# Pooled attention and two MLPs: half of the plain products, a turn on VectorE and a shorter warm-up in group 0

## The chip, the cores and the metric

One core of a Trainium2 chip runs the whole program in one launch. The metric is the device time in microseconds (us), the median of several runs; three runs of the kernel before are shown. An engine is named by its profile name: PE is TensorE, DVE VectorE, ACT ScalarE, POOL GpSimd, SP SyncE, whose queue issues the DMAs.

## The reference

Inputs are float64 arrays. Attention has 8 batches, 8 heads, 576 positions and 64 columns; k and v are averaged over blocks of 8 positions, so 72 keys stay per head. Its output, 4608 rows of 512, goes through two MLPs with 2048 hidden columns:

```python
k_p = k.reshape(B, H, Sp, pool, D).mean(axis=3)
v_p = v.reshape(B, H, Sp, pool, D).mean(axis=3)
scores = scale * np.matmul(q, k_p.transpose(0, 1, 3, 2))
attn = np.exp(scores - np.max(scores, axis=-1, keepdims=True))
attn = attn / (np.sum(attn, axis=-1, keepdims=True) + 1e-09)
x = np.matmul(attn, v_p)
...
h = x @ w_in
g = h * (1.0 / (1.0 + np.exp(-h)))
x = g @ w_out
...
h = x @ w_in2
g = h * np.clip(h + 3.0, 0.0, 6.0) / 6.0
out = g @ w_out2
```

## The kernel before, in words

The 4608 rows are 36 tiles of 128 (TPG = 4 to a group), 9 groups of 512 (NG). The hidden columns are 16 slices of 128 (NF). The first MLP runs group by group and, in a group, slice by slice; one pass of that loop is called a slot here, slot f of group g. Everything is written in the order in which each engine executes it (manual_schedule); engines wait for each other only by data and buffers.

A slot of the first MLP does h_mm (L489: twelve products of 128x512, since x and the weight are each held as a high and a low part), the activation act_a (L507: tanh on ACT, then one DVE pass), and y_mm of the slice before (L546: twelve products again, high and low parts). For that, act_b (L523) splits g into gh (ACT) and gl (DVE). In group 0 the kernel takes another way for y: g and the weight of w_out stay whole in float32, and y_whole (L536) does four plain float32 products; the weights of w_out are then split in group 1 by split_whole (L137).

The weights arrive as float64. split_a (L101) makes a float32 of each: ACT copies, then DVE does a shift and one or two passes of two operands; with mul the last step is POOL's and ACT adds a sign. split_b (L144) makes the high part (ACT) and the low part (POOL subtracts). There are 32 pieces, w_in and w_out of each slice in turn; five are converted before slot 0, and this table says how many in each slot:

```python
share = [2, 2, 2] + [1, 3, 2] * 4 + [2]
```

In a slot, one conversion stands right behind act_a and the rest of the quota further back, behind y_mm and ahead of norm in program order (L862, L864).

The attention of the next group's four tiles runs in the slots of a group; stages (L670) says where. Step 1 is scores (L349, PE), below_max (DVE), exps (ACT) and, late in the slot, norm (L403, DVE). The probabilities must then be turned so that keys stand on partitions. In group 0 step 2, a slot later, is probs_T (L414): eight PE transposes and two ACT copies. In all later groups step 4 in the slot of the scores is vector_T (L431): three DVE transposes of 32x32 blocks, a write of 384 KB to DRAM and three reads back in the order wanted; SP issues them at the start of the next slot (the list later). Step 3 is weighted (L456, PE) and split_x: two slots behind the scores in group 0, three in the others. In group 0 the scores stand in slots 3, 6, 9 and 12 (tiles 4 to 7), in later groups in slots 0, 4, 8, 12.

pool_k (L277, DVE) and pool_v (L297, POOL) add up blocks of 8; batch 1's k, which tile 4 needs, is pooled in slots 0 to 2. The buffer of v serves for the turned blocks too (tag v).

Before slot 0 the four tiles of group 0 go through attention alone. PE first runs products on zeros: warm_wide (L332), 14 of 128x512, 10 of 128x256 and 10 with another stride, then keep_warm with WARM[t], pairs of 128x128 ahead of the scores and the transposes. The second MLP runs after all groups of the first; the change does not touch it.

Of the kernel before, what the change touches and what calls it, by code (L numbers as in the profile page):

```python
# [18 lines left out]

POOL = 8  # L20
GT = 512
WARM = (12, 5, 3, 3)


@with_exitstack
def kernel(
# [14 lines left out]
    nc = tc.nc  # L41
# [8 lines left out]
    TPG = GT // P  # L50
# [50 lines left out]
    def split_a(layer, f, piece, mul=False):  # L101


        raw = w_raw.pop((layer, f, piece))
        hw = raw[:, :, 1]

        dst = raw[:, :, 1] if piece else None
        mag = att.tile([P, DM], F32, tag="wmag", name="wmag", bufs=4)
        bits = mag.bitcast(U32)
        nc.scalar.activation(mag, hw.bitcast(F32), AF.Copy, scale=2.0 ** -112)  # L110
        if mul:
            nc.scalar.activation(hw.bitcast(F32), hw.bitcast(F32), AF.Sign)
        nc.vector.tensor_scalar(
            out=bits, in0=bits, scalar1=3, scalar2=None, op0=ALU.logical_shift_left
        )
        nc.vector.scalar_tensor_tensor(
            out=bits, in0=raw[:, :, 0], scalar=29, in1=bits,
            op0=ALU.logical_shift_right, op1=ALU.bitwise_or,
        )
        if mul:  # L120
            nc.gpsimd.tensor_tensor(
                out=mag if dst is None else dst.bitcast(F32), in0=mag, in1=hw.bitcast(F32),
                op=ALU.mult,
            )
        else:
            nc.vector.scalar_tensor_tensor(
                out=bits if dst is None else dst, in0=hw, scalar=0x80000000, in1=bits,
                op0=ALU.bitwise_and, op1=ALU.bitwise_or,
            )
        if piece:  # L130
            w_whole[f] = dst.bitcast(F32)
        else:
            w_mag[layer, f, piece] = mag

    w_whole = {}

    def split_whole(f):  # L137

# [193 lines left out]
    def warm_wide(ps):  # L332

        w = probe[:, :P]
        for n in range(14):
            nc.tensor.matmul(ps, w, shuffled(probe), start=True, stop=True)
        for n in range(10):
            nc.tensor.matmul(ps[:, :256], w, shuffled(probe[:, :256]), start=True, stop=True)
        for n in range(10):
            nc.tensor.matmul(  # L340
                ps, w, probe.rearrange("p (a f) -> p f a", a=4), start=True, stop=True
            )

    def keep_warm(ps, n):

# [158 lines left out]
                )  # L504
        return ps

    def act_a(g, ps):  # L507


        t = p2.tile([P, GT], F32, tag="t", name="t")  # L510
        if g == 0:
            nc.scalar.activation(in_two(t), dealt(ps), AF.Tanh, scale=0.5)
            nc.vector.scalar_tensor_tensor(
                out=in_two(t), in0=in_two(t), scalar=1.0, in1=dealt(ps), op0=ALU.add, op1=ALU.mult
            )
            return t
# [19 lines left out]
    def y_whole(f):  # L536
# [3 lines left out]
            y_ps[0, 0] = [ps_y.tile([P, 512], F32, tag=f"y{i}", name=f"y{i}") for i in range(4)]  # L540
        for i, ps in enumerate(y_ps[0, 0]):
            nc.tensor.matmul(  # L542
                ps, w[:, i * P:(i + 1) * P], shuffled(t), start=(f == 0), stop=(f == NF - 1)
            )

    def y_mm(layer, g, f):  # L546
        if (layer, g) == (0, 0):
            return y_whole(f)
        gh, gl = g_t.pop((layer, g, f))
        oh, ol = w_sl[layer, f, 1]  # L550
# [119 lines left out]
    def stages(g):  # L670
        d = [[] for _ in range(NF)]
        if g + 1 < NG:
            for i in range(TPG):
                s = 3 + 3 * i if g == 0 else 4 * i
                t = TPG * (g + 1) + i
                d[s].append((1, t))
                if g == 0:
                    d[s + 1].append((2, t))
                    d[s + 2].append((3, t))
                else:  # L680
                    d[s].append((4, t))
                    d[s + 3].append((3, t))
        return d


# [6 lines left out]
    with tc.manual_schedule():  # L692
# [105 lines left out]
        for layer in range(1):  # L798
            for g in range(NG):
# [4 lines left out]
                for f in range(NF):  # L804
# [5 lines left out]
                            load_half(*ahead2.pop(0))  # L810
                    while later:
                        later.pop(0)()
                    if g == 1:
                        split_whole(f)
                    ps = h_mm(layer, g, f)
                    if 1 in now:
# [3 lines left out]
                            load_q(t1 + 1)  # L820
                    if 3 in now:
                        pv = weighted(now[3])
                    tt = act_a(g, ps)
                    quota = share[n] if n < NF else 2
                    due = len(done)
                    conv_a(1, 0)
                    for job in jobs_b:
                        job()
                    jobs_b = []
                    if g:  # L830
                        act_b(layer, g, f, tt)
                    else:
                        g_t[0, 0, f] = tt
                    if NF <= n < (NG - 1) * NF and SPLITTING[f] and jobs:
                        key, jobs_b = jobs.pop(0)
                        if key:
# [12 lines left out]
                        exps(t1, 1)  # L849
                    if 3 in now:  # L850
                        split_x(now[3], pv)
                    if n < 3:
                        for j in ((0, 1), (2,), (3,))[n]:
                            pool_k(1, j)
                    if 1 <= n < 5:
                        pool_v(1, n - 1)
                    if pend is not None:
# [6 lines left out]
                        norm(t1)  # L864
                    if 4 in now:
                        vector_T(now[4])
                    if 2 in now:
                        probs_T(now[2])
                    if n >= 5 and f % 2 == 1:
                        for b, j in kv_wait:  # L870
                            pool_k(b, j)
                            pool_v(b, j)
                        kv_wait = []
                        if kv_jobs and f % 4 == 1 and TPG * (g + 1) + f // 4 + 4 >= first_tile[kv_jobs[0][0]]:
                            b, j = kv_jobs.pop(0)
                            load_k(b, j)
                            load_v(b, j)
# [142 lines left out]
```

## Time and profile before

| what | value |
|---|---|
| median of 3 runs | 1624.27 us (1624.21 to 1625.08) |
| the profiled execution, its own time | 1624.84 us |
| its span, first to last instruction | 1623.1 us |
| mean granted clock of TensorE | 0.997 |
| PE busy | 1596.5 us (98%) |
| DVE busy | 987.2 us (61%) |
| ACT busy | 632.4 us (39%) |
| POOL busy | 367.3 us (23%) |
| group 0, first slice's h product to group 1's first | 33.49 to 166.56 us |

The shares are means over the whole span. Group 0 is 133 us of 1623 and has another mix of work than the rest: there the weights are converted. A clock of 1.00 in a row is 2.4 GHz, 0.50 is 1.2 GHz. In a timeline, equal instructions that follow each other stand in one row with their count; a plain float32 product counts twice.

### The profile page before, as it was taken

Reading aid. Unit: us, or ns where it says so; the run is one execution under the profiler, and the core shown is the slowest. Engines: PE = TensorE matmul, PEld = TensorE weight load, DVE = VectorE, ACT = ScalarE, POOL = GpSimd, SP = SyncE. Lnnn points to the kernel's source line nnn. Section 1 sums busy time; section 2 is a strip of 40 time slices with the busy share of each in tenths; the row PEclk is TensorE's granted clock in tenths of the full one; section 3 lists DMA queues with packets and bytes.
Section 4 is the critical chain, followed back from the end, with each engine's and each line's share of the span. In section 5 each row is a group of like instructions: output and inputs, shape, how many; then the busy total and the mean of one; then the engine's idle time right before and its main releaser. Section 6 shows DMA issues by size and latency. Waiting matters only on the chain.

```text
span 1623.1 us, 24092 instructions
## 1 busy us (share of the span) xinstructions
PE 1596.5 (98%) x9248; PEld 1390.3 (86%) x9248; DVE 987.2 (61%) x1592; ACT 632.4 (39%) x1094; POOL 367.3 (23%) x377
## 2 busy tenths in 40 slices
PE   7899999999999999999999999999999999999999
PEld 6455788888888888888888899999999999999998
DVE  6986666676676666765532555555556565656464
ACT  5443564333333333333322333343434343334333
POOL 4643353122312231311011021202030302020200
PEclk9899999999999999999999999999999999999999
DMA  9351245254443444343155634343434343534341
GB/s 295 133 191 41 97 149 161 93 161 148 142 136 123 159 154 132 128 131 125 67 196 206 221 110 156 112 156 104 156 104 157 104 165 96 169 100 160 104 131 53
DMA packets 101331, 224.27 MB, mean 138 GB/s; under 512 B 10464, under 2 KB 35936, under 8 KB 101216
## 3 DMA queue, kind: packets, MB, share of 16 engines
q1 hardware_dynamic: 101216, 222.73, 42.1%
q8 instruction: 73, 1.20, 0.3%
q14 instruction: 42, 0.34, 0.1%
HBM read 169.74 MB, written 52.95 MB: 137 GB/s over the span
## 4 chain that ended last, share of the span: by engine, by line
PE 87%; DVE 6%; DMA 3%; ACT 2%; issue 1%; SPq 0%; ACTq 0%; DVEq 0%
PE y L562 41%; PE hps L498 22%; PE p L637 16%; PE y L542 4%; PE aps L359 2%; PE aps L463 2%; DVE u L909 1%; ACT gh L660 1%; DVE gl L661 1%; DVE t L653 1%; ACT t L652 1%; DVE o L574 1%; DMA wraw<-in_moe_w_out_dram 1%; DMA stage<-in_v_dram 1%; DMA qT<-in_q_dram 1%
## 5 line engine op out<-in xcount | busy, mean ns | idle before, releaser
L498 PE MATMUL hps<-x,whl 128*128 128x512 f32 x1728 | 404.8, 384 | 4.2 <-POOL whl L151 2.1
L498 PEld LDWEIGHTS hps<-x,whl 128*128 128x128 f32 x1728 | 327.1, 190 | 59.3 <-issue 8.0
L637 PEld LDWEIGHTS p<-xst,wst 128*128 128x128 f32 x3024 | 359.6, 192 | 15.0 <-DVE u L909 7.8
L637 PE MATMUL p<-xst,wst 128*128 128x256 f32 x3024 | 363.1, 275 | 4.6 <-DVE u L909 4.6
L562 PE MATMUL y<-whl,gh 128*128 128x512 f32 x1152 | 343.1, 379 | 0.6 <-ACT gh L660 0.6
L562 PE MATMUL y<-gh,whl 128*128 128x512 f32 x1024 | 310.0, 384 | 0.0
L562 PEld LDWEIGHTS y<-whl,gh 128*128 128x128 f32 x1152 | 207.3, 190 | 24.1 <-ACT gh L660 0.8
L625 POOL TENSOR_TENSOR xst<-xr,xst 128x512 fp32r<-128x512 f32 x63 | 83.5, 1327 | 619.1 <-ACT xst L624 579.3
L562 PE MATMUL y<-whl,gl 128*128 128x512 f32 x576 | 218.4, 379 | 0.1
L562 PEld LDWEIGHTS y<-gh,whl 128*128 128x128 f32 x1024 | 189.4, 189 | 29.4 <-issue 3.1
L661 DVE TENSOR_TENSOR gl<-t,gh 128x512 fp32r<-128x512 f32 x144 | 115.4, 802 | 131.5 <-ACT gh L660 131.5
L562 PE MATMUL y<-gl,whl 128*128 128x512 f32 x512 | 194.6, 380 | 0.0
L518 DVE SCALAR_TENSOR_TENSOR hps<-t,hps 128x512 f32<-128x512 f32 x128 | 88.2, 689 | 169.0 <-ACT t L517 168.5
L517 ACT ACTIVATE t<-hps 128x512 f32<-128x512 f32 x128 | 76.3, 596 | 263.7 <-PE hps L498 262.1
L660 ACT ACTIVATE gh<-t 128x512 fp32r<-128x512 f32 x144 | 120.4, 836 | 127.1 <-DVE t L653 127.1
L193 POOL TENSOR_TENSOR hs<-hmag,hs 128x256 fp32r<-128x256 f32 x88 | 64.2, 734 | 410.4 <-ACT hs L192 380.8
L653 DVE SCALAR_TENSOR_TENSOR t<-t,u 128x512 f32<-128x512 f32 x108 | 90.9, 841 | 105.0 <-ACT t L652 105.0
L909 DVE TENSOR_TENSOR u<-u,p 128x512 f32<-128x512 f32 x180 | 120.4, 685 | 43.9 <-PE p L637 39.8
L652 ACT ACTIVATE t<-u,three 128x512 f32<-128x512 f32 x108 | 77.8, 720 | 171.7 <-DVE u L909 171.7
L527 DVE TENSOR_TENSOR gl<-hps,gh 128x512 fp32r<-128x512 f32 x128 | 88.5, 691 | 85.1 <-ACT gh L526 85.1
L526 ACT ACTIVATE gh<-hps 128x512 fp32r<-128x512 f32 x128 | 76.6, 598 | 125.3 <-DVE hps L518 125.3
L562 PEld LDWEIGHTS y<-whl,gl 128*128 128x128 f32 x576 | 108.9, 189 | 15.9 <-DVE gl L661 0.5
(95 smaller groups left out, 1455.0 us busy)
## 6 DMA issues: line engine op xcount, KB each, us to landing
wst<-ws SPq DMA_DIRECT2D x156, 512.0 KB
ws<-hs SPq DMA_DIRECT2D x56, 256.0 KB
bl<-bT SPq DMA_DIRECT2D x28, 384.0 KB
x<-o SPq DMA_DIRECT2D x36, 256.0 KB
xr<-x SPq DMA_DIRECT2D x36, 256.0 KB
out_dram<-o SPq DMA_DIRECT2D x36, 256.0 KB
wraw<-in_moe_w_in_dram SPq DMA_DIRECT2D x16, 512.0 KB
wraw<-in_moe_w_out_dram SPq DMA_DIRECT2D x16, 512.0 KB
```

The costliest lines, as they stand in the source:

```text
L498: nc.tensor.matmul(ps, w[:, c, :], shuffled(x[:, c, :]), start=(c == 0 and n == 0), stop=(c == NKC - 1 and n == 2),)
L518: nc.vector.scalar_tensor_tensor(out=ps, in0=t, scalar=1.0, in1=ps, op0=ALU.add, op1=ALU.mult)
L526: nc.scalar.activation(in_two(gh), dealt(ps), AF.Copy)
L527: nc.vector.tensor_tensor(out=in_two(gl), in0=dealt(ps), in1=in_two(gh).bitcast(F32), op=ALU.subtract)
L562: nc.tensor.matmul(ps, a, shuffled(b), start=(f == FIRST[layer] and n == 0), stop=(f == LAST[layer] and n == 2),)
L625: nc.gpsimd.tensor_tensor(out=t[:, 1], in0=src, in1=t[:, 0].bitcast(F32), op=ALU.subtract)
L637: nc.tensor.matmul(ps[:, j * HW:(j + 1) * HW], w[:, j, a, c, :], shuffled(x[:, b, c, :]), start=(j == 0 and n == 0 and c == 0), stop=(j == ...
L652: nc.scalar.activation(t, h, AF.Relu, bias=three)
L653: nc.vector.scalar_tensor_tensor(out=t, in0=t, scalar=6.0, in1=h, op0=ALU.min, op1=ALU.mult)
L660: nc.scalar.activation(oh, t3, AF.Copy)
L661: nc.vector.tensor_tensor(out=ol, in0=t3, in1=oh.bitcast(F32), op=ALU.subtract)
L909: nc.vector.tensor_tensor(out=out, in0=a, in1=b, op=ALU.add)
```

## The change

Four edits. (1) The plain float32 y is kept for slices 0 to 7 only; slices 8 to 15 of group 0 are split like those of later groups (split_a, act_a, act_b, y_mm), and split_whole in group 1 has eight slices. (2) The attention that runs in group 0 moves one slot back (scores in 4, 7, 10, 13; batch 1's k pooled in slots 0 to 3) and is turned by vector_T in the slot of the scores; step 2 and its transposes are gone, the weighted sum stays two slots behind the scores. (3) k and v of later batches are loaded in slots 5, 8, 11, 14 of group 0 and pooled in the slot after, four loads where there were three. (4) warm_wide has 24 wide products, and the 10 narrow, the 10 of another stride and the 12 pairs ahead of the first scores are gone. The table share is as it was.

```diff
-WARM = (12, 5, 3, 3)
+WARM = (0, 5, 3, 3)
...
-        dst = raw[:, :, 1] if piece else None
+        whole = piece and f < NWHOLE
+        dst = raw[:, :, 1] if whole else None
...
-        if piece:
+        if whole:
             w_whole[f] = dst.bitcast(F32)
         else:
             w_mag[layer, f, piece] = mag
 
     w_whole = {}
+    NWHOLE = NF // 2
...
-        for n in range(14):
+        for n in range(24):
             nc.tensor.matmul(ps, w, shuffled(probe), start=True, stop=True)
-        for n in range(10):
-            nc.tensor.matmul(ps[:, :256], w, shuffled(probe[:, :256]), start=True, stop=True)
-        for n in range(10):
-            nc.tensor.matmul(
-                ps, w, probe.rearrange("p (a f) -> p f a", a=4), start=True, stop=True
-            )
...
     def y_mm(layer, g, f):
-        if (layer, g) == (0, 0):
+        if f in w_whole:
             return y_whole(f)
...
-                s = 3 + 3 * i if g == 0 else 4 * i
+                s = 4 + 3 * i if g == 0 else 4 * i
                 t = TPG * (g + 1) + i
                 d[s].append((1, t))
-                if g == 0:
-                    d[s + 1].append((2, t))
-                    d[s + 2].append((3, t))
-                else:
-                    d[s].append((4, t))
-                    d[s + 3].append((3, t))
+                d[s].append((4, t))
+                d[s + (3 if g else 2)].append((3, t))
...
-                    if g == 1:
+                    if g == 1 and f in w_whole:
                         split_whole(f)
...
-                    tt = act_a(g, ps)
+                    whole = g == 0 and f < NWHOLE
+                    tt = act_a(whole, ps)
...
-                    if g:
+                    if whole:
+                        g_t[0, 0, f] = tt
+                    else:
                         act_b(layer, g, f, tt)
-                    else:
-                        g_t[0, 0, f] = tt
...
-                    if n < 3:
-                        for j in ((0, 1), (2,), (3,))[n]:
-                            pool_k(1, j)
+                    if n < 4:
+                        pool_k(1, n)
...
-                    if 2 in now:
-                        probs_T(now[2])
-                    if n >= 5 and f % 2 == 1:
+                    if n >= 5 and (f % 3 == 0 if n < NF else f % 2 == 1):
                         for b, j in kv_wait:
                             pool_k(b, j)
                             pool_v(b, j)
                         kv_wait = []
-                        if kv_jobs and f % 4 == 1 and TPG * (g + 1) + f // 4 + 4 >= first_tile[kv_jobs[0][0]]:
+                    if n >= 5 and (f % 3 == 2 if n < NF else f % 4 == 1):
+                        if kv_jobs and TPG * (g + 1) + f // 4 + 4 >= first_tile[kv_jobs[0][0]]:
```

On DVE, where the maxima of tile 5 (pr_85) go over into its normalisation; before:

```order
L376 TENSOR_TENSOR pr_85<-aps,mx 128x288
L407 TENSOR_REDUCE den<-pr_85 128x8
L408 TENSOR_SCALAR den<-den 128x8
L411 RECIPROCAL den<-den 128x8
L412 TENSOR_TENSOR pr_85<-pr_85,den 128x576
L513 SCALAR_TENSOR_TENSOR t<-t,hps 128x512
```

and with the change (line numbers move by two or three: L376 is now L373, L113 is now L115):

```order
L373 TENSOR_TENSOR pr_85<-aps,mx 128x288
L115 TENSOR_SCALAR wmag<-wmag 128x512
L118 SCALAR_TENSOR_TENSOR wmag<-wraw,wmag 128x512
L115 TENSOR_SCALAR wmag<-wmag 128x512
L118 SCALAR_TENSOR_TENSOR wmag<-wraw,wmag 128x512
L128 SCALAR_TENSOR_TENSOR wmag<-wraw,wmag 128x512
L404 TENSOR_REDUCE den<-pr_85 128x8
L405 TENSOR_SCALAR den<-den 128x8
L408 RECIPROCAL den<-den 128x8
L409 TENSOR_TENSOR pr_85<-pr_85,den 128x576
L437 STREAM_TRANSPOSE bT<-pr_85 128x256 x3
```

Two conversions (L115 to L128) now stand between the maxima and the normalisation, and the turn (L437) behind it.

On PE, from the turned tile 5 to the scores of tile 6; before:

```order
L423 MATMUL aps<-ident,pr_85 72x128 x8
L498 MATMUL hps<-x,whl 128x512 x12
L463 MATMUL aps<-pT,vp_83 64x128 x8
L542 MATMUL y_597<-t,wraw 128x512
L542 MATMUL y_598<-t,wraw 128x512
L542 MATMUL y_599<-t,wraw 128x512
L542 MATMUL y_600<-t,wraw 128x512
L498 MATMUL hps<-x,whl 128x512 x12
L359 MATMUL aps<-kbd_81,qT 128x144 x4
```

and with the change, where y takes eight rows of twelve products in place of four rows of plain float32:

```order
L495 MATMUL hps<-x,whl 128x512 x12
L460 MATMUL aps<-pT,vp_83 64x128 x8
L559 MATMUL y_573<-gh,whl 128x512 x2
L559 MATMUL y_573<-gl,whl 128x512
L559 MATMUL y_574<-gh,whl 128x512 x2
L559 MATMUL y_574<-gl,whl 128x512
L559 MATMUL y_575<-gh,whl 128x512 x2
L559 MATMUL y_575<-gl,whl 128x512
L559 MATMUL y_576<-gh,whl 128x512 x2
L559 MATMUL y_576<-gl,whl 128x512
L495 MATMUL hps<-x,whl 128x512 x12
L356 MATMUL aps<-kbd_81,qT 128x144 x4
```

The transposes (L423) are gone, and one slice pair stands between the weighted sum (L460) and the scores (L356), as before.

On SP, around the trip of tile 5's turned blocks (bl_96); before, from the weights of the same time:

```order
L98 DMA wraw<-in_moe_w_out_dram 128x1024
L98 DMA wraw<-in_moe_w_in_dram 128x1024
L98 DMA wraw<-in_moe_w_out_dram 128x1024 x2
L321 DMA qT<-in_q_dram 128x512
L266 DMA kraw<-in_k_dram 128x576
L274 DMA vraw<-in_v_dram 72x1024
L321 DMA qT<-in_q_dram 128x512
L266 DMA kraw<-in_k_dram 128x576
L274 DMA vraw<-in_v_dram 72x1024
```

and with the change:

```order
L98 DMA wraw<-in_moe_w_in_dram 128x1024
L98 DMA wraw<-in_moe_w_out_dram 128x1024
L442 DMA bl_96<-bT 128x768
L446 DMA pT<-bl_96 32x4x256 x2
L446 DMA pT<-bl_96 8x4x256
L269 DMA kraw<-in_k_dram 128x576
L277 DMA vraw<-in_v_dram 72x1024
L98 DMA wraw<-in_moe_w_out_dram 128x1024
```

The write (L442) and its three reads stand behind the next slot's weights and ahead of the next k and v.

## Rows read from the trace of the kernel before

**Rows 1.** stretches: us, busy us of each engine (instructions), clock, DMA

```profile
14.00:33.50 19.50, 14.84 (x153) 13.15 (x151) 16.06 (x38) 13.77 (x51) 6.88 (x9) 1.00 0.94 313
33.50:66.00 32.50, 22.66 (x78) 13.77 (x78) 31.18 (x35) 18.01 (x27) 20.16 (x17) 0.92 0.46 171
...
90.00:152.00 62.00, 62.00 (x236) 36.39 (x234) 52.84 (x79) 26.81 (x49) 25.20 (x19) 1.00 0.29 99
...
66.00:71.00 5.00, 4.99 (x7) 2.12 (x8) 4.90 (x6) 0.00 (x0) 3.73 (x3) 0.50 0.59 211
```

**Rows 2.** timeline, PE, group 0: start, us, operation, [idle before <- releaser]

```profile
66.01 0.74 PE L359 MATMUL aps<-kbd,qT 128*64 128x144 f32 x2 [5.40 <-DVE kbd L290]
66.68 6.21 PE L542 MATMUL y<-t,wraw 128*128 128x512 f32 x8
...
83.20 1.15 PE L463 MATMUL aps<-pT,vp 72*64 72x64 f32 x32
84.28 4.59 PE L542 MATMUL y<-t,wraw 128*128 128x512 f32 x8
...
91.30 1.14 PE L359 MATMUL aps<-kbd,qT 128*128 128x144 f32 x8
92.28 4.48 PE L542 MATMUL y<-t,wraw 128*128 128x512 f32 x8
...
170.64 4.48 PE L542 MATMUL y<-t,wraw 128*128 128x512 f32 x8
```

**Rows 3.** timeline, PE then VectorE: warm-up, first scores, their last pooled k

```profile
7.37 1.28 PE L338 MATMUL aps<-probe 128*128 128x256 f32 x10
...
14.00 4.09 PE L359 MATMUL aps<-kbd,stage 128*128 128x144 f32 x32
...
8.69 1.51 DVE L290 TENSOR_REDUCE kbd<-stage 64x72 f32<-64x576 f32 x2 [1.79 <-DMA stage<-in_k_dram]
```

**Rows 4.** timeline, PE, group 1: h products, one slot apart

```profile
180.13 2.75 PE L498 MATMUL hps<-x,whl 128*128 128x512 f32 x12
...
185.31 2.75 PE L498 MATMUL hps<-x,whl 128*128 128x512 f32 x12
```

**Rows 5.** timeline, VectorE, first conversion of slot 3

```profile
70.55 1.64 DVE L126 SCALAR_TENSOR_TENSOR wmag<-wraw,wmag 128x512 uint32<-128x512 uint32 x1
```

**Rows 6.** timeline, VectorE, tile 5: maxima, sums, end of normalisation

```profile
95.48 0.45 DVE L375 TENSOR_REDUCE mx<-aps 128x4 f32<-128x288 f32 x1
...
97.78 0.75 DVE L407 TENSOR_REDUCE den<-pr 128x8 f32<-128x576 f32 x1 [0.51 <-ACT pr L383]
...
99.01 0.76 DVE L412 TENSOR_TENSOR pr<-pr,den 128x576 f32<-128x576 f32 x1
```

**Rows 7.** groups by line: | busy us, mean ns | idle before, releasers

```profile
L110 ACT ACTIVATE wmag<-wraw 128x512 f32<-128x512 f32 x32 | 22.1, 691 | 2.1 <-POOL wraw L121 2.1
L151 POOL TENSOR_TENSOR whl<-wcopy,whl 128x512 fp32r<-128x512 f32 x16 | 21.8, 1360 | 56.6 <-ACT whl L150 56.6
...
L423 PE MATMUL aps<-ident,pr 128*72 128x128 f32 x32 | 4.1, 272 | 0.0
```

**Rows 8.** timeline, VectorE, group 0: two conversions, twice

```profile
103.37 0.41 DVE L113 TENSOR_SCALAR wmag<-wmag 128x512 uint32<-128x512 uint32 x1
...
106.74 1.64 DVE L126 SCALAR_TENSOR_TENSOR wraw<-wraw,wmag 128x512 uint32<-128x512 uint32 x1
...
127.19 0.41 DVE L113 TENSOR_SCALAR wmag<-wmag 128x512 uint32<-128x512 uint32 x1
127.64 0.69 DVE L116 SCALAR_TENSOR_TENSOR wmag<-wraw,wmag 128x512 uint32<-128x512 uint32 x1
...
130.56 0.73 DVE L126 SCALAR_TENSOR_TENSOR wraw<-wraw,wmag 128x512 uint32<-128x512 uint32 x1
```

**Rows 9.** timeline, VectorE then SyncE, group 1: turn, reads back

```profile
177.83 1.10 DVE L440 STREAM_TRANSPOSE bT<-pr 128x256 f32<-128x256 f32 x3
...
181.34 1.19 SPq L449 DMA_DIRECT2D pT<-bl  x3
```

More of the change, by code (lines that the diff above doesn't have):

```diff
@@ L505, in h_mm, with act_a @@
         return ps
-    def act_a(g, ps):
+    def act_a(whole, ps):
         t = p2.tile([P, GT], F32, tag="t", name="t")
-        if g == 0:
+        if whole:
             nc.scalar.activation(in_two(t), dealt(ps), AF.Tanh, scale=0.5)
@@ L542, in y_whole @@
             nc.tensor.matmul(
-                ps, w[:, i * P:(i + 1) * P], shuffled(t), start=(f == 0), stop=(f == NF - 1)
+                ps, w[:, i * P:(i + 1) * P], shuffled(t), start=(f == 0), stop=False
             )
     def y_mm(layer, g, f):
-        if (layer, g) == (0, 0):
+        if f in w_whole:
             return y_whole(f)
@@ L673, in stages @@
             for i in range(TPG):
-                s = 3 + 3 * i if g == 0 else 4 * i
+                s = 4 + 3 * i if g == 0 else 4 * i
                 t = TPG * (g + 1) + i
                 d[s].append((1, t))
-                if g == 0:
-                    d[s + 1].append((2, t))
-                    d[s + 2].append((3, t))
-                else:
-                    d[s].append((4, t))
-                    d[s + 3].append((3, t))
+                d[s].append((4, t))
+                d[s + (3 if g else 2)].append((3, t))
         return d
@@ L829 @@
                     jobs_b = []
-                    if g:
+                    if whole:
+                        g_t[0, 0, f] = tt
+                    else:
                         act_b(layer, g, f, tt)
-                    else:
-                        g_t[0, 0, f] = tt
                     if NF <= n < (NG - 1) * NF and SPLITTING[f] and jobs:
```

## The prediction

> **What bounds the kernel now.** I read the stretches first, by stage, to see which engine is full where [rows 1]. From 33.5 to 66 us VectorE (DVE) is busy for 31.18 of 32.5 us and TensorE (PE) for 22.66: the first slots of group 0 wait for VectorE. From 90 to 152 us, the rest of group 0's conversions, PE is full (62.00 of 62.00) and VectorE has only 9 us to spare. So in group 0 PE sets the pace today, and VectorE stands right behind it. Next I read PE's own order in time in group 0 [rows 2]: one old slice is twelve products for h and eight passes for the plain y, 84.28 to 91.30, 7.02 us; scores cost 0.98 (91.30 to 92.28) and the weighted sum 1.08 (83.20 to 84.28). PE waits 5.40 us once, ahead of the last two score products of tile 4, for a pooled k of VectorE. From the y after tile 4's scores (66.68) to the y after tile 8's (170.64) are 103.96 us; that stretch is the one that the change rebuilds.
>
> **The change, part by part.**
>
> *Warm-up.* Tile 0's scores start at 14.00 because PE works through its list of warm-up products until then; the pooled k that they read is there at 8.69 + 1.51 = 10.20 [rows 3]. The new list is the same 14 wide products to 7.37 and ten more at 0.216 us (a slice pair of group 1, 24 products in 5.18 us [rows 4]), so to 9.5. The scores then start at about 10.3: **-3.7 us**. Bounds: -3.8, if nothing else waits, and 0, if a later load sets the prologue anyway; I take -3.7, since VectorE and ScalarE follow the scores directly.
>
> *Pooled k one slot later.* The last pooling of batch 1 moves from slot 2 to behind the first conversion of slot 3. VectorE has no slack there, so the same instructions must be done by then: it ends where that conversion ends now, 70.55 + 1.64 = 72.19 [rows 5], less 3.7, so 68.5. Two more score products (0.67) follow, and y after tile 4's scores starts at 69.2 instead of 66.68: **+2.5 us**. PE does one more slice pair ahead of them, which takes the place of the time gained; the wait of some 5 us and the lower clock behind it stay.
>
> *Turning.* Now PE transposes in the next slot and ScalarE copies; both go away. Instead VectorE turns the probabilities at the end of the scores' own slot, and they go out to DRAM and back before PE may take the weighted sum two slots on. What stands on that path, from the end of the scores, for tile 5 [rows 6]: 3.20 until VectorE comes to the maxima (95.48 - 92.28); maxima and subtraction 1.79; then, new on this path, conversions. The table of conversions per slot is unchanged and gives the old scores' slots (3, 6, 9, 12) one conversion, the new ones (4, 7, 10, 13) three, and two of these stand ahead of the normalisation in VectorE's order. VectorE waits 0.51 for the exponentials today and will wait 0.69 more for ScalarE's copy [rows 7]: 1.20. Two conversions took 4.10 us in one stretch and 5.01 in another, where GpSimd pools v beside them (the last pass of the second one is 0.73 alone and 1.64 beside GpSimd) [rows 8]; the new slots have GpSimd's extra subtractions beside them but no pooling, so I take the middle, 4.55. Normalisation 1.99 (97.78 to 99.77). The turn 1.10 (to 178.93); the reads back are issued at 181.34, when the write has landed, 2.41 later, and I count the same again for the reads, which carry less: 4.82 [rows 9]. Sum of the path: **18.7 us**. On SyncE's queue the write now waits for VectorE, and behind it stand the next k and v, q of the next tile and the weights of slots to come; those are converted two slots later or more, so I cost it at nothing; without that cover a conversion would start late, which is more of what C prices.
>
> The Trainium skill ("DMA: Bandwidth & Descriptors", section "Anatomy of one DMA") puts a fixed cost of about 2.0 us on each transfer plus its bytes at 436 GB/s, fitted on another issuing path. By it the two hops would be an estimated 5.6 us and the whole sum below some 3 us higher; the row's 2.41 for the larger hop is under the page's 2.9, and the row decides.
>
> PE's own work between scores and weighted sum is two slice pairs: 2 x 7.02 = 14.0 for tile 5, 2 x 5.18 = 10.4 for tiles 6 and 7, whose slices are the cheaper kind [rows 2, 4]. The path is longer than both. So **PE waits for the turned tile** in all four rounds, and a round lasts as long as the path plus what PE does from the weighted sum to the next scores:
>
> - tile 4 to 5: 18.7 + (92.28 - 83.20 = 9.08) = 27.8
> - tile 5 to 6: 18.7 + (1.08 + 5.18 + 0.98 = 7.24) = 25.9, and the clock
> - tile 6 to 7: one subtraction for gl more on VectorE ahead of the maxima (0.6): 26.5, and the clock
> - tile 7 to 8: only one conversion is left, of the kind that GpSimd ends (1.14 on VectorE [rows 8]): 26.5 - 3.4 = 23.1, and the clock.
>
> The clock: behind the wait of 5.40 us the granted clock is 0.50 (the level of 1.2 GHz) from 66 to 71 us while PE works [rows 1], which loses 2.5 us. The waits that come out here are 18.7 - 14.0 = 4.7, 19.3 - 10.4 = 8.9 and 15.9 - 10.4 = 5.5; I take 2.5 for each, 7.5 in all. Bounds: 0 and 10, if tile 4's shorter wait drops it too. Sum: 27.8 + 28.4 + 29.0 + 25.6 = 110.8 against 103.96: **+6.8 us**.
>
> *Split y.* Eight slices of 7.02 become 5.18 on PE. Seven of them lie inside the rounds above and are counted there; the last stands behind tile 8's scores: **-1.8 us**. Its price is a subtraction for gl, ScalarE's copies and GpSimd's subtractions in slots 8 to 15; group 1 loses eight copies in turn, on a ScalarE that nobody waits for there.
>
> Sum: 2.5 + 6.8 - 1.8 = **+7.5 us** (the warm-up's 3.7 is in the 2.5). The profiled execution took 1624.84; 1632.3 on its scale, and, the median being 0.57 lower, **1631.8** on that of the runs. Changing kv loads to every third slot costs PE nothing here: their poolings stand in slots without scores. Crosswise: PE loses 3.7 + 4.1 (transposes [rows 7]) + 8 x 1.84 = 22.5 us of work and gains waits of 2 to 9 us four times, and the slower clock: about as much again and some more.
>
> **Rivals.**
>
> *A, PE stays the bound, faster.* If the turned tile came back within PE's two slices, the 22.5 us would stand as a gain: 1602. In its favour: in later groups the same trip hides, with three slots between turn and use. Against: here it has less than two, and two conversions stand ahead of the normalisation. It needs a path under 10.4 us; 18.7 is the sum of rows. Chance 0.07.
>
> *B, no change.* The path holds but the waits don't lower the clock: 1631.8 - 7.5 = 1624.3. In its favour: from 14 to 33.5 us PE was idle for nearly 5 us in short pieces at a clock of 1.00 [rows 1]. It decides if 5 to 9 us of waiting count like those; the one wait of 5.40 did not. Chance 0.10.
>
> *C, much slower.* GpSimd's eight new subtractions (1.36 each [rows 7]) fall on the conversions inside the path; a pass of VectorE beside GpSimd takes 0.9 longer [rows 8], two in each of three rounds: 5.5 more, 1637.3. It decides when ScalarE's copy releases them in the scores' slot. Chance 0.11. The Trainium skill ("SBUF — State Buffer", on the shared port pair) states an exclusive lock, under which the second comer waits out the other's whole instruction; by that rule the same estimate would be up to 1.36 a pass.
>
> *D, the warm-up gains nothing.* The prologue waits for loads, or the clock falls once the small products are gone: +3.7, 1635.5. Against: the last v is pooled ahead of its use today. Chance 0.07.
>
> **How the numbers follow.** My forecast has 0.65. The range goes from 1626 (the clock lost in one round instead of three) to 1639 (C with the longer conversions): B and A lie below it. A measurement of this kernel can tell about 0.2%, 3.2 us, from no change. Slower than 1627.5: the forecast, C and D, 0.82. Within: B and the short end of the forecast, 0.11. Faster: A, 0.07.
>
> **What would show it.** Right: scores of tile 0 near 10.3 us; a wait ahead of the weighted sums of tiles 4 to 7, ended by the DMA of the turned tile, 2 to 9 us, longest for tile 6; a granted clock of 0.5 behind the longer ones; group 0's last slice some 7 us later than now; groups 1 and on unchanged. Wrong: no wait ahead of those sums (A), or waits at a clock of 1.00 (B), or VectorE's conversions stretched in the scores' slots (C).

## The result and the profile after

The changed kernel takes 1642.24 us (median of 4 runs, 1641.22 to 1643.26) beside 1624.26 us of the kernel before on the same chip: **1.0109 of its time, 95% interval 1.0092 to 1.0127**, 18 us slower. The forecast was 1631.8, with a range that ended at 1639. The sign was right; less than half of the size was.

| what | before | after |
|---|---|---|
| the profiled execution, its own time | 1624.84 us | 1642.05 us |
| its span | 1623.1 us | 1640.3 us |
| mean granted clock of TensorE | 0.997 | 0.987 |
| PE busy | 1596.5 us | 1585.2 us |
| group 0, first slice's h product to group 1's first | 33.49 to 166.56 us | 31.82 to 186.9 us |

The page of the changed kernel: busy time of each engine, the granted clock in 40 slices, and the chain of waits by engine.

```profile
PE 1585.2 (97%) x9214; PEld 1396.5 (85%) x9214; DVE 998.1 (61%) x1612; ACT 627.4 (38%) x1086; POOL 365.9 (22%) x377
...
PEclk9988999999999999999999999999999999999999
...
PE 83%; DVE 9%; ACT 3%; issue 2%; DMA 1%; SPq 0%; POOL 0%; DVEq 0%; ACTq 0%; POOLq 0%
```

TensorE is busy for 11 us less and the program takes 17 us more in this execution, so waits were added; only slices 3 and 4 of the clock's row, 82 to 164 us, now stand at 8, and they lie in group 0. There PE's own order in time shows them (start, duration, operation, [idle before it <- what ended that]).

```profile
10.44 2.12 PE L356 MATMUL aps<-kbd,stage 128*128 128x144 f32 x16
13.96 1.22 PE L356 MATMUL aps<-kbd,stage 128*128 128x144 f32 x8 [1.39 <-DMA stage<-in_q_dram]
16.47 1.25 PE L356 MATMUL aps<-kbd,stage 128*128 128x144 f32 x8 [1.30 <-DMA stage<-in_q_dram]
...
31.82 2.86 PE L495 MATMUL hps<-x,whl 128*128 128x512 f32 x12 [0.86 <-ACT x L476]
...
70.70 0.74 PE L356 MATMUL aps<-kbd,qT 128*64 128x144 f32 x2 [5.38 <-DVE kbd L293]
71.37 6.42 PE L539 MATMUL y<-t,wraw 128*128 128x512 f32 x8
...
91.48 1.98 PE L460 MATMUL aps<-pT,vp 72*64 72x64 f32 x32 [4.18 <-DMA pT<-bl]
...
101.67 1.14 PE L356 MATMUL aps<-kbd,qT 128*128 128x144 f32 x8
...
122.29 1.97 PE L460 MATMUL aps<-pT,vp 72*64 72x128 f32 x16 [5.66 <-DMA pT<-bl]
...
131.11 1.14 PE L356 MATMUL aps<-kbd,qT 128*128 128x144 f32 x8
...
153.20 1.98 PE L460 MATMUL aps<-pT,vp 72*64 72x128 f32 x16 [10.58 <-DMA pT<-bl]
...
161.93 1.14 PE L356 MATMUL aps<-kbd,qT 128*128 128x144 f32 x8
...
181.00 1.97 PE L460 MATMUL aps<-pT,vp 72*64 72x128 f32 x16 [7.56 <-DMA pT<-bl]
...
189.49 1.14 PE L356 MATMUL aps<-kbd,qT 128*128 128x144 f32 x8
```

Where [rows 2] had one wait of more than 4 us in group 0, there are five. The four new ones stand ahead of the weighted sums (L460) of tiles 4 to 7, all ended by the DMA that brings the turned probabilities, 27.98 us in all. The scores of tile 5, 0.98 us, end at 102.65, those of tiles 6 to 8 by the same step at 132.09, 162.91 and 190.47. So the four rounds from tile 4's scores (71.37) last 31.28, 29.44, 30.82 and 27.56 us, 119.1 together where they had 103.96 [rows 2]. The account on the scale of the profiled execution: tile 4's scores end 4.7 later (71.37 - 66.68), the rounds are 15.1 longer, and from tile 8's scores (190.47 beside 170.64) to the end of the program 2.6 are gained: 4.7 + 15.1 - 2.6 = 17.2 = 1642.05 - 1624.84.

Stretches of the same trace (start:end, length, busy time of each engine, granted clock, DMA share, GB/s):

```profile
69.50:76.30 6.80, 5.60 (x8) 2.45 (x9) 6.62 (x10) 0.90 (x2) 5.23 (x6) 0.50 0.47 161
90.00:96.80 6.80, 5.32 (x36) 3.32 (x37) 5.32 (x6) 0.60 (x1) 3.79 (x4) 0.50 0.96 296
96.80:120.70 23.90, 19.83 (x65) 11.50 (x63) 14.89 (x26) 8.76 (x16) 6.20 (x6) 1.00 0.30 114
120.70:127.50 6.80, 5.21 (x24) 4.27 (x25) 6.70 (x7) 3.71 (x7) 5.70 (x5) 0.50 0.74 210
148.00:158.20 10.20, 5.00 (x23) 4.13 (x24) 8.77 (x11) 6.56 (x12) 7.99 (x6) 0.50 0.53 151
178.70:185.50 6.80, 4.50 (x22) 3.75 (x23) 2.54 (x4) 2.38 (x4) 2.07 (x2) 0.50 0.92 272
```

Each of the waits has a stretch at 0.50 (1.2 GHz) with it, the one of 4.18 us too, in which PE has work to do.

Tile 5's path, VectorE and then SyncE's queue:

```profile
105.84 0.45 DVE L372 TENSOR_REDUCE mx<-aps 128x4 f32<-128x288 f32 x1
...
108.92 0.43 DVE L115 TENSOR_SCALAR wmag<-wmag 128x512 uint32<-128x512 uint32 x1 [1.28 <-ACT wmag L112]
...
113.21 0.75 DVE L404 TENSOR_REDUCE den<-pr 128x8 f32<-128x576 f32 x1
...
115.28 1.10 DVE L437 STREAM_TRANSPOSE bT<-pr 128x256 f32<-128x256 f32 x3
...
116.41 0.33 SPq L442 DMA_DIRECT2D bl<-bT  x1
...
118.76 1.18 SPq L446 DMA_DIRECT2D pT<-bl  x3
```

From the end of the scores at 102.65: 3.19 to the maxima; 3.08 for maxima, subtraction and a wait of 1.28 for ScalarE's copy; two conversions 4.29; normalisation 2.07; turn 1.10 to 116.38; write to the issue of the reads 2.38 (116.38 to 118.76); reads to PE 3.53 (to 122.29). Sum 19.64; from the end of the scores to the weighted sum tile 4's path is 20.1 us, those of tiles 6 and 7 are 21.1 and 18.1. The turns of tiles 4, 6 and 7, from whose ends (85.64, 147.29, 175.20) their trips to PE are counted:

```profile
84.54 1.10 DVE L437 STREAM_TRANSPOSE bT<-pr 128x256 f32<-128x256 f32 x3
...
146.19 1.10 DVE L437 STREAM_TRANSPOSE bT<-pr 128x256 f32<-128x256 f32 x3
...
174.10 1.10 DVE L437 STREAM_TRANSPOSE bT<-pr 128x256 f32<-128x256 f32 x3
```

### The profile page after: what moved, and what is told of

The parts are those of the page before. It is cut to its first block, busy times and chain, and to the rows that moved or that the text cites. A ratio compares the mean times of both kernels' runs of the same rounds, so it can differ in the third digit from the quotient of the medians.

```text
span 1640.3 us, 24083 instructions
## 1 busy us (share of the span) xinstructions
PE 1585.2 (97%) x9214; PEld 1396.5 (85%) x9214; DVE 998.1 (61%) x1612; ACT 627.4 (38%) x1086; POOL 365.9 (22%) x377
## 4 chain that ended last, share of the span: by engine, by line
PE 83%; DVE 9%; ACT 3%; issue 2%; DMA 1%; SPq 0%; POOL 0%; DVEq 0%; ACTq 0%; POOLq 0%
PE y L559 42%; PE hps L495 21%; PE p L634 16%; PE aps L460 2%; PE aps L356 2%; DVE u L902 1%; ACT gh L657 1%; DVE gl L658 1%; DVE t L650 1%; DVE wmag L115 1%; ACT t L649 1%; DVE wmag L118 1%; DVE o L571 1%; DMA pT<-bl 1%; DMA bl<-bT 1%
## 5 line engine op out<-in xcount | busy, mean ns | idle before, releaser
L559 PE MATMUL y<-gh,whl 128*128 128x512 f32 x1088 | 333.2, 388 | 0.0
L559 PEld LDWEIGHTS y<-gh,whl 128*128 128x128 f32 x1088 | 203.3, 191 | 32.5 <-issue 4.3
L559 PE MATMUL y<-gl,whl 128*128 128x512 f32 x544 | 208.3, 383 | 0.0
L515 DVE SCALAR_TENSOR_TENSOR hps<-t,hps 128x512 f32<-128x512 f32 x136 | 93.6, 688 | 175.8 <-ACT t L514 175.2
L514 ACT ACTIVATE t<-hps 128x512 f32<-128x512 f32 x136 | 81.1, 597 | 286.6 <-PE hps L495 286.3
L524 DVE TENSOR_TENSOR gl<-hps,gh 128x512 fp32r<-128x512 f32 x136 | 94.0, 691 | 86.4 <-ACT gh L523 86.4
L523 ACT ACTIVATE gh<-hps 128x512 fp32r<-128x512 f32 x136 | 81.3, 598 | 144.7 <-DVE hps L515 144.3
```

The lines of the kernel that those rows point to most:

```text
L515: nc.vector.scalar_tensor_tensor(out=ps, in0=t, scalar=1.0, in1=ps, op0=ALU.add, op1=ALU.mult)
L523: nc.scalar.activation(in_two(gh), dealt(ps), AF.Copy)
L524: nc.vector.tensor_tensor(out=in_two(gl), in0=dealt(ps), in1=in_two(gh).bitcast(F32), op=ALU.subtract)
L559: nc.tensor.matmul(ps, a, shuffled(b), start=(f == FIRST[layer] and n == 0), stop=(f == LAST[layer] and n == 2),)
```

## The experiments

Theory of the slowdown, **PATH**: the turned tile's way (two conversions ahead of the normalisation, then the trip to DRAM and back) is longer than PE's two slice pairs, and the clock falls behind each wait. Rivals: that the split of y loads VectorE, or that the warm-up does it. Differences in us are to the kernel before on the same chip.

**1. The warm-up alone**, on the kernel before.

```diff
-WARM = (12, 5, 3, 3)
+WARM = (0, 5, 3, 3)
...
-        for n in range(14):
+        for n in range(24):
```

(and warm_wide's two other loops gone)

> The kernel before with the shorter warm-up alone. Path theory (the slow part is PE waiting for the turned tile, and the warm-up is a small gain cut short by late q loads): the first h product comes 1.67 us earlier, as in the changed kernel's trace (31.82 against 33.49), so 1622.6 us. Rival (the clock or the loads make the shorter warm-up cost something): 1624.3 or more. First forecast: 3.7 us less, 1620.6.

1622.54 us, 0.9983 of before (0.9973 to 0.9992): -2.65, the first h product at 30.55. This part gains: its whole interval lies below 1. Of the versions that compute the same result only this one and its variant in experiment 9 are shown to beat the kernel before, by 0.2% or less.

**2. The split of y for slices 8 to 15 alone**, on the kernel before: the lines with whole and NWHOLE of the change's diff.

> The kernel before with the split y of slices 8 to 15 alone, attention and warm-up as before. Path theory: PE loses up to 8 x 1.84 = 14.7 us of work, but VectorE had only 9 us to spare in 90 to 152 us and gets eight subtractions of 0.6 and more of GpSimd beside it, so most of it is not realised: 1618 to 1622 us, faster than before. Rival (the extra work on VectorE and GpSimd is itself what costs 18 us): 1630 us or more.

1624.03, 0.9992 (0.9983 to 1.0001): no change that can be told, above the expected range. PE's timeline of this run shows the longest of the waits that eat the gain:

```profile
150.61 0.80 PE L564 MATMUL y<-gl,whl 128*128 128x512 f32 x1 [4.61 <-DVE gl L529]
```

VectorE, to which each split slice gives a subtraction (gl), comes late. The split costs nothing, and here, where VectorE has little room, it gives nothing that can be told.

**3. The change, with the table of conversions moved along with the scores.**

```diff
-    share = [2, 2, 2] + [1, 3, 2] * 4 + [2]
+    share = [2, 2, 2, 2] + [1, 3, 2] * 4
```

> The changed kernel with the table of conversions moved one slot too, so that the slots of the scores have one conversion again. Path theory: two conversions (4.3 us) and 0.75 us of waiting for ScalarE's copy leave the path of three tiles, one conversion the fourth's; the waits of 4.2, 5.7, 10.6 and 7.6 us become about 0, 0.7, 5.6 and 6.3, and one or two falls of the clock (2.5 each) go: 12 to 18 us less than the change, 1624 to 1630 us. Rival (VectorE's sum of work sets the pace, wherever the conversions stand): 1640 us or more.

1634.81, 1.0058 (1.0042 to 1.0075): +9.6, so 8.4 of the 18 recovered, less than expected. Tile 5's wait fell from 5.66 to 0.50, but 3.56, 4.43 and 6.43 stayed for tiles 4, 6 and 7, and a new one of 3.94 for gl came. Tiles 6 and 7 have slices of the cheaper kind, which cover only 10.4 us of the path; tile 4's wait had been expected to go, and its write took 5.37 us here (issued at 80.93, the reads at 86.30; experiment 11 shows what moved beside it).

**4. The change, turned by PE as before** (transposes a slot behind the scores, no DRAM).

```diff
-                d[s].append((4, t))
-                d[s + (3 if g else 2)].append((3, t))
+                if g == 0:
+                    d[s + 1].append((2, t))
+                    d[s + 2].append((3, t))
+                else:
+                    d[s].append((4, t))
+                    d[s + 3].append((3, t))
```

(and the call of probs_T back in the slot's order)

> The changed kernel with the turn back on PE and ScalarE a slot behind the scores; all else, the slots and the split y too, as changed. Path theory: the trip through DRAM (5.9 us) is gone, what is left of the path ends ahead of the transposes or a few us behind them: 1619 to 1627 us. Rival (the split's extra work, not the trip, is the cost): 1635 us or more.

1628.29, 1.0018 (1.0009 to 1.0027): +3.1. Without the way over DRAM 14.9 of the 18 us come back, though the conversions still stand ahead of the normalisation. What is left of the waits is theirs: PE's transposes of tile 6 wait for the normalisation behind them.

```profile
137.70 1.68 PE L420 MATMUL aps<-ident,pr 128*72 128x128 f32 x7 [6.00 <-DVE pr L409]
```

**5. The change without the split** (plain y for all sixteen slices).

```diff
-    NWHOLE = NF // 2
+    NWHOLE = NF
```

> The changed kernel with all sixteen slices of group 0 in the plain float32 way again; slots, turn and warm-up as changed. Path theory: the path of the turned tile is what it was (20.1, 19.6, about 20.5 and 17.5 us, the subtraction for gl gone), so a round is the path plus 9.1 us of dearer PE work plus the clock; PE's cover is longer (14.0 instead of 10.4 us), so the waits for tiles 6 and 7 shrink to about 6.5 and 3.5 us, but no round gets shorter: the same as the change or up to 6 us more, 1641 to 1648 us. Rival (the split's work on VectorE and GpSimd is the cost): 1635 us or less.

1646.54, 1.0133 (1.0118 to 1.0148): +21.3, as PATH expected. The split is not what slows the kernel; the waits for tiles 4 to 7 are 4.29, 6.67, 6.78 and 3.17 us. PE has more work under the same path, and still waits.

**6. Without the split and with the table moved** (the edits of 3 and 5).

> The same with the table of conversions moved one slot as well. Path theory: the path is about 14.6 us, PE's cover 14.0; waits of 0 to 2.5 us, no lower clock behind most, the transposes' 3.2 us gone and the warm-up's gain in: 1619 to 1625 us, at or below the kernel before. Rival (VectorE's sum of work): 1630 us or more.

1626.94, 1.0013 (1.0004 to 1.0022): +1.7, above the expected range by 2. Three waits are under 1 us (0.45, 0.90, 0.77), since plain slices cover 14.0 us in every round; tile 4's stays at 4.23, of which experiment 11 says more.

**7. PE's turn and the moved table together** (the edits of 3 and 4).

> The changed kernel with the turn on PE again and the table of conversions moved one slot. In the run with the turn on PE and the table unmoved PE still waited 1.3, 6.0 and 4.0 us for the normalisation. Path theory: those waits stem from the two conversions ahead of it and fall to about 2 us or less: 1618 to 1623 us. Rival (moving the slots costs by itself): 1628 us as with the table unmoved.

1623.67, 0.9992 (0.9982 to 1.0001): back at the kernel before within the measure. No wait for a turned tile is left, but two for gl (3.73 and 4.61), as in the split alone.

**8. The change with only VectorE's order altered**: normalisation and turn ahead of the conversions of their slot.

```diff
-                    conv_a(quota - 1, 1)
                     if 1 in now:
                         norm(t1)
                     if 4 in now:
                         vector_T(now[4])
+                    conv_a(quota - 1, 1)
```

> The changed kernel, its table of conversions unmoved, but in each slot the second and third conversion are written behind normalisation and turn instead of ahead of them: VectorE does the same work in the same slot. Path theory: 4.4 + 0.75 us leave the path of tiles 4 to 6 and about 2 us that of tile 7; waits of 0, 0.5, 5.5 and 5.5 us are left, as with the moved table (1634.8): 1628 to 1636 us. Rival (VectorE's sum sets the pace): 1640 us or more.

1627.94, 1.0016 (1.0007 to 1.0026): +2.7, at the low end of what was expected. One line moved gives 15.3 of the 18 us back. PE's timeline:

```profile
86.07 1.15 PE L460 MATMUL aps<-pT,vp 72*64 72x64 f32 x32 [0.73 <-DMA pT<-bl]
...
109.71 1.09 PE L460 MATMUL aps<-pT,vp 72*64 72x128 f32 x16 [0.57 <-DMA pT<-bl]
...
121.27 0.76 PE L356 MATMUL aps<-kbd,qT 128*128 128x144 f32 x4 [4.13 <-DVE x L477]
...
137.12 1.09 PE L460 MATMUL aps<-pT,vp 72*64 72x128 f32 x16 [3.05 <-DMA pT<-bl]
...
148.63 0.76 PE L356 MATMUL aps<-kbd,qT 128*128 128x144 f32 x4 [2.44 <-DVE x L477]
...
164.64 1.09 PE L460 MATMUL aps<-pT,vp 72*64 72x128 f32 x16 [3.20 <-DMA pT<-bl]
```

The waits for the turned tiles fall from 27.98 to 7.55 us, and the weighted sums behind them run in 1.09 to 1.15 us where they took 1.97 or 1.98 at the lower clock. The conversions that were pushed back now delay VectorE's split of x (L477), for which the next scores wait: part of the stall moved. This settles PATH: the conversions and the trip are what the change added to the path, and with either one off it (here and in experiment 4) most of the time comes back. The two gains, 15.3 and 14.9, are not parts of one sum: each shortens the same waits.

**9 and 10. Why the short warm-up gave less than 3.7 us.** The scores began at 10.44 as forecast, but the first h product came only 1.67 us earlier. Two theories: late loads of q (the waits of 1.39 and 1.30 above), or VectorE. In run 9, on the warm-up alone, the loads of q go ahead of three loads of v:

```diff
-        for t in range(1, TPG):
-            load_v(0, t - 1, f"i{NF - 5 + t}")
-            load_q(t, f"i{4 + t}")
-        load_v(0, NPAIR - 1, f"i{NF - 1}")
+        for t in range(1, TPG):
+            load_q(t, f"i{4 + t}")
+            if t == 1:
+                load_v(0, 0, f"i{NF - 4}")
+        for j in range(1, NPAIR):
+            load_v(0, j, f"i{NF - 4 + j}")
```

> The kernel before with the short warm-up, and in the prologue the loads of q of tiles 2 and 3 issued ahead of the last three loads of v. Two theories of why the short warm-up moved the first h product by 1.7 us (changed kernel) and 2.9 us (warm-up alone) and not by 3.7. Q LOADS: the scores of tiles 2 and 3 wait 1.2 and 1.3 us for q, and that delay reaches the end; then those waits go, and the first h product comes 1.3 to 2.5 us earlier than the 30.55 of the run with the warm-up alone, at 28.0 to 29.3; time some 2 us below that run's. VECTORE: the maxima start 3.6 us earlier, as forecast, and from there to the first conversion VectorE has hardly a wait, but runs more of its passes beside GpSimd's pooling of v (15.8 us there instead of 15.2 before, 17.1 in the changed kernel); then the q waits go and the first h product stays within 0.7 us of 30.55.

```profile
9.54 4.08 PE L353 MATMUL aps<-kbd,stage 128*128 128x144 f32 x32
...
30.77 2.86 PE L492 MATMUL hps<-x,whl 128*128 128x512 f32 x12 [0.86 <-ACT x L473]
```

The four tiles' scores run without a wait and end 3.9 us earlier than in experiment 1, and the first h product stays where it was (30.77 beside 30.55). Time 1621.85, 0.9988 (0.9979 to 0.9997), like the warm-up alone. The late loads of q were not what held it. In run 10 GpSimd's pooling of v is left out (ones in its place):

```diff
+        nc.gpsimd.memset(vp[0], 1.0)
         pool_k(0, 3, nc.gpsimd)
         for j in range(NPAIR):
-            pool_v(0, j)
+            kv_raw.pop((0, j, "v"))
```

> The kernel before with the short warm-up, and GpSimd's pooling of v of batch 0 left out: the tile of pooled v is filled with ones instead, so the attention of tiles 0 to 3 is that of other values. VECTORE theory: VectorE's stretch from the first maxima to the first conversion loses what is longer beside GpSimd there (in the run with the warm-up alone: 0.53 on a short operation, 0.84 on two normalisations, 0.15 on another, 1.5 us in all), so 15.8 becomes about 14.3 us, and the first h product comes at about 29.0 instead of 30.55; time some 1.5 us below that of the warm-up alone. Q LOADS theory: the first h product stays at 30.5, since the loads of q stand where they were.

Groups by line, VectorE, from the first maxima on (busy us, mean ns | idle before): first two rows of the changed kernel,

```profile
L409 DVE TENSOR_TENSOR stage<-stage,den 128x576 f32<-128x576 f32 x2 | 2.4, 1194 | 0.1
L387 DVE TENSOR_SCALAR mx<-mx 128x4 f32<-128x4 f32 x4 | 2.3, 582 | 0.1
```

then of this run.

```profile
L406 DVE TENSOR_TENSOR stage<-stage,den 128x576 f32<-128x576 f32 x2 | 1.5, 758 | 0.1
...
L384 DVE TENSOR_SCALAR mx<-mx 128x4 f32<-128x4 f32 x4 | 0.7, 170 | 0.1
```

With GpSimd silent the same two operations take 758 ns and 170 ns instead of 1194 and 582. So that part of VectorE's theory is shown: the pooling lengthens its operations. But the first h product came at 31.41, not at 29.0. PE's and ScalarE's timelines and a stretch of this run say why.

```profile
16.06 2.03 PE L353 MATMUL aps<-kbd,stage 128*128 128x144 f32 x8 [1.21 <-DMA stage<-in_q_dram]
...
19.91 1.04 PE L417 MATMUL aps<-ident,stage 128*72 128x128 f32 x8
```

```profile
20.54 1.08 ACT L418 ACTIVATE pT<-aps 72x512 f32<-72x512 f32 x2 [5.63 <-PE aps L417]
```

```profile
16.40:19.80 3.40, 3.40 (x18) 3.40 (x17) 3.11 (x9) 0.00 (x0) 0.00 (x0) 0.50 1.02 398
```

In this execution the granted clock was 0.50 from 16.4 to 19.8 us, after PE had waited for q three times; the first transposes came at 19.91, ScalarE waited 5.63 us for them and VectorE 2.19 for ScalarE. PE, at the lower clock, became the bound here. So no run shows that the first h product comes earlier once the pooling is gone. Time 1621.93, 0.9981 (0.9972 to 0.9990), no better than the warm-up alone.

**11. Experiment 6 with the order of 8** (the edits of 3, 5 and 8), meant to beat all.

> The changed kernel with the normalisation and the turn ahead of the two conversions in VectorE's order, the table of conversions moved with the scores to slots 4, 7, 10 and 13, and y left plain for all sixteen slices. Without the order change this took 1626.9 with a wait of 4.2 us for the turned tile 4 and waits under 1 us for the others. Theory: the order takes some 3.4 us off the path of tile 4, as it did with the split (4.2 to 0.7), and the clock's fall behind that wait goes with it (2.1): 1626.9 - 3.4 - 2.1 = 1621.4; waits for the turned tiles under 1 us in all four rounds. 1619 to 1623.5; below the 1622.5 of the best so far if it all comes. Rival: the conversions pushed behind the turn are late for their own slices, and VectorE's split of x comes late for the next scores, as with the split: waits there of 2 to 4 us, 1624 to 1629.

1626.76, 1.0015 (1.0006 to 1.0024), what experiment 6 gave: the theory's 3.4 us did not come, nor did the rival. The expectation had overlooked that with the moved table a slot with scores has one conversion, so the line that moves asks for none: the edit changes nothing, and the run repeats experiment 6 with the same program. It leaves the question why tile 4's path is long in both. In experiment 6 SyncE's queue shows it:

```profile
80.71 0.33 SPq L442 DMA_DIRECT2D bl<-bT  x1
86.53 1.20 SPq L446 DMA_DIRECT2D pT<-bl  x3
```

and two stretches, from the write's issue to that of the reads: first of experiment 6, then of the changed kernel.

```profile
80.70:86.50 5.80, 5.03 (x17) 2.85 (x15) 5.66 (x8) 2.37 (x5) 2.53 (x2) 1.00 0.80 296
```

```profile
85.70:88.00 2.30, 1.60 (x8) 1.06 (x6) 2.23 (x4) 0.67 (x2) 0.00 (x0) 1.00 0.42 171
```

The write lands after 5.8 us instead of 2.38. In the changed kernel 171 GB/s x 2.3 us = 0.39 MB pass in that time, the write itself; here 296 x 5.8 = 1.7 MB: besides the write, weights and q, whose loads SyncE issued from 76.48 to 78.7. In experiment 8 tile 4's write went at 78.14 and the reads at 82.69, 4.55 later. An early turn runs into the loads that a late one found finished. That a later issue of those loads would mend it was not tried.

**12. The warm-up and the split together**, on the kernel before (the edits of 1 and 2).

> The kernel before with two of the change's parts, the short warm-up and the split of y's second half of slices; no turn, scores where they were. Alone the first gave -2.7 us and the second -1.2 us (no change within the measure). If they add: 1624.3 - 3.9 = 1620.4. Rival: VectorE, the bound from the first slots on, takes the second's gain away again once it runs earlier: 1622.5, as the warm-up alone. 1620 to 1623.

1622.93, 0.9993 (0.9984 to 1.0002): they don't add, as the rival had it; the wait for gl at 150.43 is 4.60 us again. In the profiled execution the clock fell early in the prologue (0.50 from 17.4 to 20.8 us) and the first h product came at 32.98.

The change's other edits, the later slots and the loads of k and v in every third slot, were not run by themselves. Experiment 7 has them and the moved table on top of these two parts, and gives -1.57 beside -1.66 here: together they cost nothing that can be told.

## Why the prediction was wrong, by its own steps

**What held.** PE waits for the turned tile in all four rounds and the clock falls behind the waits; a round is path plus PE's part. The pieces of VectorE came out as summed: for tile 5 3.19 to the maxima (forecast 3.20), 1.28 of waiting (1.20), conversions 4.29 (4.55), normalisation 2.07 (1.99), turn 1.10. SyncE's queue cost nothing in the changed kernel, as costed: tile 5's write was issued 0.03 us behind the turn.

On the profiled execution's scale the forecast was +7.5 and the measured difference +17.2. The 9.7 us between them:

- **The trip to DRAM, +4.2.** The step that failed first: "and I count the same again for the reads, which carry less: 4.82". The write took 2.38, as its row said [rows 9], but the reads took 3.53 from their issue to PE, and the four trips 5.84, 5.91, 5.91 and 5.80. That size had no row of its own, and it was given no bound. Part of it stood in the row that was used: three reads take 1.19 us to issue, one behind the other [rows 9], so the last of them goes out some 0.8 us behind the first, while the write is one issue. The Trainium skill ("DMA: Bandwidth & Descriptors", section "Anatomy of one DMA") gave an estimated 5.6 us for both hops, nearer than the row that was put above it; yet its single hops, 2.9 and 2.7 by the same estimate, agree with neither 2.38 nor 3.53.
- **The warm-up, +2.0.** Tile 0's scores began at 10.44, near the 10.3 of the forecast, but partly by luck: pooled k was there at 9.63, and PE's longer list held them, its 24 products taking 8.26 us in this execution (7.24 in that of experiment 8). "VectorE and ScalarE follow the scores directly" was right for the start (first maxima 11.13 instead of 14.69, -3.56) and wrong for the length: from there to the first conversion VectorE took 17.06 us (to 28.19) instead of 15.16 (14.69 to 29.85), because those passes now run beside GpSimd's pooling of v, which had been half done by then. In VectorE's rows, of the changed kernel and then of the kernel before:

```profile
11.13 0.46 DVE L372 TENSOR_REDUCE mx<-aps 128x4 f32<-128x288 f32 x1 [1.50 <-PE aps L356]
...
28.19 0.43 DVE L115 TENSOR_SCALAR wmag<-wmag 128x512 uint32<-128x512 uint32 x1 [0.32 <-ACT wmag L112]
```

```profile
14.69 0.46 DVE L375 TENSOR_REDUCE mx<-aps 128x4 f32<-128x288 f32 x1 [4.49 <-PE aps L359]
...
29.85 0.43 DVE L113 TENSOR_SCALAR wmag<-wmag 128x512 uint32<-128x512 uint32 x1 [0.32 <-ACT wmag L110]
```

Against the times of experiment 10, without the pooling, the operations in this stretch are longer by 2.78 us in all, and by 0.88 in the kernel before; the difference is the 1.90 between 17.06 and 15.16. How much it takes differs between executions. Experiments 6 and 11 are one program, and their first h products came at 30.23 and 31.75; that of experiment 8, with the same prologue, came at 29.85, 3.64 earlier than in the kernel before. So the 2.0 is the size in this execution, not a fixed price. The Trainium skill ("SBUF — State Buffer", section "SBUF: two separate sides") lets a VectorE pass of some kinds and a GpSimd instruction exclude each other for a whole instruction; an operation of 170 ns that takes up to 1.11 us beside adds of 0.72 to 1.27 us agrees. I had used that rule for conversions only, in C.

- **The clock, +1.9.** I took 2.5 for three rounds and none for tile 4. PE's parts of the rounds were 11.17, 9.80, 9.71 and 9.47 against 9.08 and three times 7.24 at full clock: 9.4 us lost, near the bound of 10 that I had named for the case that tile 4's wait counts too. It did. The prediction's own sum gave tile 4 the same wait as tile 5 (18.7 - 14.0 = 4.7), and it had no reason on record for counting the one fall and not the other.
- **Maxima and small operations, +2.2.** Tiles 6 and 7 came to their maxima 4.54 and 4.21 us after the scores, not 3.8, and for tiles 4 and 7 one short operation of the normalisation took 0.78 and 0.76 instead of 0.17.
- **Behind tile 8, -0.8**: 2.6 gained where 1.8 was forecast. What the 0.8 comes from was not taken apart. The rest, 0.2, lies ahead of tile 4's scores.

**The rivals.** A (PE stays the bound) would have needed a path under 10.4; it was 18.1 to 21.1. B (waits that leave the clock alone) did not happen: every one had its stretch at 0.50. C (GpSimd's subtractions on the path) did not either: the two conversions of tiles 4, 5 and 6 took 4.48, 4.29 and 4.43 us, all less than the 4.55 of the forecast. D was half right in its size, 2.0 of 3.7, for a reason it did not name; of its two, loads were not what held the first h product in experiment 9, and the fall of the clock was seen in experiments 5, 10 and 12, not in the changed kernel's profile.

**The range** ended at 1639 because C was its far end. Four paths that share one step share its error: 1 us on the trip is 4 us on the sum, and no case held that.

## What to carry to other kernels

Before moving a result onto a longer way, add up that way from the engine's order and set it against the work that covers it; here the path was 20 us over a cover of 10 to 14, and putting the urgent step ahead of work that is due later was worth 15 us, even though that work then came late in two places. A step that is repeated in every round needs bounds of its own, and a hop timed by the next instruction's issue is not a hop timed by its consumer. And a stage that starts earlier may meet a neighbour that it used to miss: look at what runs beside it at the new time.

## What the runs showed that was not expected

- Three reads that carry less than the write take longer to their consumer: 3.53 us from issue to PE, 2.38 from write to the reads' issue. Some 0.8 us of it passes before the last of the three is issued; what the rest is stays open, for no run took it apart.
- The same write takes 2.38 us with no load still moving and 4.55 to 5.8 with up to 1.3 MB of loads moving beside it.
- VectorE's operation on 128x4 elements took 0.17 to 1.11 us beside GpSimd's adds; with these gone all four took 0.17.
- The warm-up's list made no difference to the clock in the changed kernel's prologue (1.00 from 14 to 33 us), but in the profiled executions of experiments 5, 10 and 12 the clock was 0.50 there for a while, so single executions of such a kernel differ by a few us ahead of the first slot: the twelve with the short warm-up have their first h product between 29.85 and 34.29 us.
